# A gated recurrence and a long convolution on one core: scan on transposed inputs, 128x49 prime-factor convolution, batches overlapped

## The chip, the cores and the metric

The kernel runs on one core of one Trainium2 chip. The metric is the device time of a launch in microseconds (us). The times are medians of four executions (three in the first table of the kernel before); each execution also lists the core's span (from its first to its last instruction) and its mean granted TensorE clock, as a share of full speed. Engines: PE is TensorE, PEld its weight loads, DVE VectorE, ACT ScalarE, POOL GpSimd, SP SyncE.

## The reference

```python
# x, f_logit: (4, 6272, 256) f32; the weights are shared by the batches
f = lower_bound + (1 - lower_bound) * sigmoid(f_logit)
for t in range(6272):                      # recurrence in time
    h = f[:, t] * h + (1 - f[:, t]) * x[:, t]
    y[:, t] = h
x1, x2, x3 = split(y @ w_proj, 3)          # 256 columns each
conv = irfft(rfft(x2, axis=1) * rfft(filter_fft, axis=0))   # circular, length 6272
out = (x1 * conv * x3) @ w_out
```

6272 is 128 x 49, and 128 and 49 have no common factor. A Fourier transform of that length can therefore be done as a 128-point and a 49-point one, either with "twiddle" factors between them (Cooley-Tukey, the kernel before) or with the time index permuted and no twiddles (Good-Thomas, the change).

## The kernel before

Four batches, one after another, each in three stages. Recurrence: a chunk of 128 time steps is a cumulated product and a cumulated sum, done as triangular matmuls around Ln and Exp.

```python
def stage0(c):                  # cumulated log f, in both orientations
    nc.tensor.matmul(pL[:, 0, :], tri16n[:], logf_c, start=True, stop=True)
    nc.tensor.matmul(pL[:, 1, 0:128], logf_c[:, 0:128], tri16[:], start=True, stop=True)
    ...
def stage1(c):
    nc.scalar.activation(cc[:], pLs.pop(c)[:], AF.Exp)
    nc.vector.tensor_tensor(g[:], us[c], cc[:, 0, :], op=AOP.mult)
def stage2(c):
    nc.tensor.matmul(pP[:, 0:128], g[:, 0:128], tri32[:], start=True, stop=True)
    ...
        nc.vector.scalar_tensor_tensor(hT[j][:, c * T:(c + 1) * T], in0=pP[:, ...],
            scalar=sc, in1=cum[:, ...], op0=AOP.add, op1=AOP.mult)
    if c in seg:                # strided permutation of h
        nc.scalar.copy(hTp[kh][:, :, k0:k1],
                       hT[kh].rearrange("p (n1 e) -> p e n1", e=N2)[:, :, k0:k1])
```

Convolution, for each half of the channels: projection x2, 128-point transform with twiddles, PE transposes, 49-point transform, product with the filter's spectrum H, PE transposes, and the way back. Then gates and output.

```python
for j in range(2):
    ... # pj = x2 projection, pA = 128-point transform with twiddle tables
    for k1 in range(g0, g0 + gn):
        nc.tensor.transpose(pT[:98, k1 - g0, :], A_sb[:, :, :, k1], iden16[:])
    ... # pX = 49-point transform; six DVE operations a group for Y = X * H
    for k1 in range(g0, g0 + gn):
        nc.tensor.transpose(pT[:98, k1 - g0, :], Y[:, k1, :, :], iden16[:])
    for dl in range(g0, g0 + GD):
        nc.tensor.matmul(pB[:NK, dl - g0, :], Yt[:98, :, dl], W49I_hi[:98, :], ...)
    ... # pc: 128-point inverse, two matmuls for each of 49
for q0 in range(0, N2, 4):      # gates: 8 matmuls of 512 columns a group and half
    ...
for sb0 in range(NCH):          # output projection, 49 stores of 128 KB a batch
    ...
    nc.sync.dma_start(out[b, sb0::N2, :], osb[:])
```

Each stage opens its own pools of SBUF and PSUM and closes them, so a stage can begin only when the memory that it needs has been given back.

Of the kernel before, what the change touches and what calls it, by code (L numbers as in the profile page):

```python
# [9 lines left out]
F32 = mybir.dt.float32  # L11
# [3 lines left out]
AF = mybir.ActivationFunctionType  # L15

S = 6272
D = 256
N1 = 128
N2 = 49  # L20
NK = 65
T = 128
NCH = S // T
DJ = 768

_DBG = None
_NB = None


def _frac_sin(nc, pool, out_ap, psum_ap, denom, pi_col, npart, nfree):  # L30
    q = pool.tile([128, nfree], F32, tag="tg_q", name="tgq")
    nc.vector.tensor_scalar(q[:npart], in0=psum_ap, scalar1=1.0 / denom,
                            scalar2=None, op0=AOP.mult)
    qi = pool.tile([128, nfree], I32, tag="tg_qi", name="tgqi")
    nc.vector.tensor_copy(qi[:npart], q[:npart])
    qf = pool.tile([128, nfree], F32, tag="tg_qf", name="tgqf")
    nc.vector.tensor_copy(qf[:npart], qi[:npart])
    r = pool.tile([128, nfree], F32, tag="tg_r", name="tgr")
    nc.vector.scalar_tensor_tensor(r[:npart], in0=qf[:npart], scalar=-float(denom),
                                   in1=psum_ap, op0=AOP.mult, op1=AOP.add)  # L40
    f0 = pool.tile([128, nfree], F32, tag="tg_f0", name="tgf0")
    nc.vector.tensor_scalar(f0[:npart], in0=r[:npart], scalar1=1.0 / denom,
                            scalar2=None, op0=AOP.mult)
    f1 = pool.tile([128, nfree], F32, tag="tg_f1", name="tgf1")
    nc.vector.scalar_tensor_tensor(f1[:npart], in0=f0[:npart], scalar=0.0,
                                   in1=f0[:npart], op0=AOP.is_lt, op1=AOP.add)
    nc.scalar.activation(out_ap, f1[:npart], AF.Sin, bias=pi_col[:npart],
                         scale=(-2.0 * math.pi))
# [3 lines left out]
def kernel(  # L52
# [13 lines left out]
    if _NB is not None:  # L66
        B = _NB
    dbg = _DBG if _DBG is not None else {}

    konst = ctx.enter_context(tc.tile_pool(name="konst", bufs=1))  # L70
    tblp = ctx.enter_context(tc.tile_pool(name="tblp", bufs=1))
    hpool = ctx.enter_context(tc.tile_pool(name="hpool", bufs=1))

    tri32 = konst.tile([128, 128], F32, tag="tri32")
    make_upper_triangular(nc, tri32, 1.0, diag=True)
    tri16 = konst.tile([128, 128], F16, tag="tri16")
    nc.vector.tensor_copy(tri16[:], tri32[:])
    tri16n = konst.tile([128, 128], F16, tag="tri16n")
    nc.vector.tensor_scalar(tri16n[:], in0=tri32[:], scalar1=-1.0, scalar2=None,
                            op0=AOP.mult)  # L80
    iden16 = konst.tile([128, 128], F16, tag="iden16")
    make_identity(nc, iden16)
    pi_col = konst.tile([128, 1], F32, tag="pi_col")
    nc.vector.memset(pi_col, math.pi)

    lbrow = konst.tile([128, D], F32, tag="lbrow")
    nc.sync.dma_start(lbrow, lower_bound.unsqueeze(0).to_broadcast([128, D]))
    onemlb = konst.tile([128, D], F32, tag="onemlb")
    nc.vector.tensor_scalar(onemlb[:], in0=lbrow[:], scalar1=-1.0, scalar2=1.0,
                            op0=AOP.mult, op1=AOP.add)  # L90

    wp_hi = konst.tile([128, 2, DJ], F16, tag="wp_hi")
    wp_lo = konst.tile([128, 2, DJ], F16, tag="wp_lo")
    wo_hi = konst.tile([128, 2, D], F16, tag="wo_hi")
    wo_lo = konst.tile([128, 2, D], F16, tag="wo_lo")

    TBLA_hi = tblp.tile([128, N2, 130], F16, tag="TBLA_hi")
    TBLAI = tblp.tile([128, N2, 2, 128], F16, tag="TBLAI")
    W49F_hi = tblp.tile([128, 98], F16, tag="W49F_hi")
    W49F_lo = tblp.tile([128, 98], F16, tag="W49F_lo")  # L100
    W49I_hi = tblp.tile([128, 98], F16, tag="W49I_hi")
    W49I_lo = tblp.tile([128, 98], F16, tag="W49I_lo")
    H_sb = [hpool.tile([128, NK, N2, 2], F16, name=f"H_{j}", tag=f"H_{j}")
            for j in range(2)]

    with tc.tile_pool(name="t32", bufs=1) as t32p:
        TBLA32 = t32p.tile([128, N2, 130], F32, tag="TBLA32")
        W49F_f32 = t32p.tile([128, 98], F32, tag="W49F_f32")
        iden32 = t32p.tile([128, 128], F32, tag="iden32")
        make_identity(nc, iden32)  # L110
        wtmp = t32p.tile([128, 2, DJ + D], F32, tag="wtmp")
        nc.sync.dma_start(wtmp[:, :, 0:DJ], moe_w_proj.rearrange("(a p) j -> p a j", p=128))
        nc.sync.dma_start(wtmp[:, :, DJ:], moe_w_out.rearrange("(a p) j -> p a j", p=128))
        nc.vector.tensor_copy(wp_hi[:], wtmp[:, :, 0:DJ])
        nc.vector.tensor_copy(wo_hi[:], wtmp[:, :, DJ:])
        nc.vector.tensor_tensor(wp_lo[:], wtmp[:, :, 0:DJ], wp_hi[:], op=AOP.subtract)
        nc.vector.tensor_tensor(wo_lo[:], wtmp[:, :, DJ:], wo_hi[:], op=AOP.subtract)

        with tc.tile_pool(name="tgen", bufs=2) as tg, \
                tc.tile_pool(name="tgen1", bufs=1) as tg1, \  # L120
                tc.tile_pool(name="tgps", bufs=2, space=bass.MemoryType.PSUM) as tgps:
            def irow(n, pattern, base, name):
                t_i = tg1.tile([1, n], I32, name=name + "_i", tag=name + "_i")
                nc.gpsimd.iota(t_i[:], pattern=pattern, base=base, channel_multiplier=0)
                t_f = tg1.tile([1, n], F32, name=name + "_f", tag=name + "_f")
                nc.vector.tensor_copy(t_f[:], t_i[:])
                return t_f
            krow = irow(130, [[0, 2], [1, NK]], 0, "krow")
            orow = irow(130, [[1568, 2], [0, NK]], 1568, "orow")
            arow = irow(128, [[49, 128]], 0, "arow")  # L130
            ones256 = irow(256, [[0, 256]], 1, "ones256")
            ones128 = ones256[:, 0:128]
            ones98 = ones256[:, 0:98]
            for g0 in range(0, N2, 3):
                gn = min(3, N2 - g0)
                pv = tgps.tile([128, 3, 130], F32, tag="tgp", name="pv")
                for jj in range(gn):
                    n2 = g0 + jj
                    bcrow = tg.tile([1, 130], F32, tag="bcrow", name="bcrow")
                    nc.vector.scalar_tensor_tensor(bcrow[:], in0=krow[:], scalar=float(n2),  # L140
                                                   in1=orow[:], op0=AOP.mult, op1=AOP.add)
                    nc.tensor.matmul(pv[:, jj, :], arow[:], krow[:], start=True, stop=False)
                    nc.tensor.matmul(pv[:, jj, :], ones128[:], bcrow[:], start=False,
# [350 lines left out]
```

## Time and profile before

| | us |
|---|---|
| median of 3 runs | 2099.86 (2098.29 to 2106.0) |
| set-up (tables, filter spectrum) | 301 |
| a batch: recurrence, convolution with gates, output | 154 + 228 + 59 = 441, with joins 451 |

The prediction below shows the lines that carry this. The page also has a row for each engine with its busy share in 40 equal slices, in tenths. In these two rows of the kernel before the reader sees four blocks apart from one another: POOL works only where a recurrence runs; ACT reaches 6 or 7 in each of them and is mostly at 0 to 3 between (with a 5 or 6 now and then).

```profile
ACT  1000027671620356762321367635122476724203
POOL 0000023300000043200000063000000333000000
```

### The profile page before, as it was taken

The page shows a single profiled execution, that of the slowest core. Times are in us where ns is not written, and L with a number is a line of the kernel's source. Part 1 is how long each engine was busy: PE and PEld are TensorE (multiplying, and loading weights), DVE is VectorE, ACT ScalarE, POOL GpSimd, SP SyncE. Part 2 cuts the span into 40 slices and gives each one's busy share as a digit, 9 for nine tenths or more (in the row PEclk, how much of TensorE's full clock was granted, in tenths as well). Part 3 has the DMA queues.
Part 4 walks back from the last instruction along what each step waited for, and adds up shares of the span by engine and source line. Part 5 has one row for each costly group of instructions (what it writes and reads, how often), then busy time and mean ns, then how long its engine had stood idle before and what let it go on. Part 6 is the DMA issues. An engine that isn't in the chain of part 4 may idle for free.

```text
span 2097.7 us, 23892 instructions
## 1 busy us (share of the span) xinstructions
PE 1407.8 (67%) x8944; PEld 1081.2 (52%) x8944; DVE 1020.8 (49%) x2697; ACT 800.7 (38%) x1364; POOL 227.4 (11%) x68
## 2 busy tenths in 40 slices
PE   5869853566979624577889334578797335679795
PEld 5547553446765313456674233457664234467643
DVE  7744616637267036626465055553752156273660
ACT  1000027671620356762321367635122476724203
POOL 0000023300000043200000063000000333000000
PEclk9995655677758955686759856786678566867597
DMA  0021022200000342100001521000002421000003
GB/s 23 0 69 54 0 94 72 80 1 1 1 1 1 108 141 80 41 1 1 1 1 35 167 86 61 21 1 1 1 1 78 151 80 61 1 1 1 1 11 113
DMA packets 92549, 86.22 MB, mean 41 GB/s; under 512 B 3984, under 2 KB 92176, under 8 KB 92432
## 3 DMA queue, kind: packets, MB, share of 16 engines
q1 hardware_dynamic: 92432, 84.69, 12.6%
q8 instruction: 70, 1.15, 0.2%
q14 instruction: 47, 0.39, 0.1%
HBM read 58.98 MB, written 25.69 MB: 40 GB/s over the span
## 4 chain that ended last, share of the span: by engine, by line
PE 32%; ACT 23%; DVE 21%; issue 12%; DMA 10%; POOL 1%; ACTq 0%; SPq 0%; DVEq 0%; POOLq 0%
DMA out_dram<-osb 7%; DVE g L271 6%; ACT Th L409 6%; PE px L431 4%; ACT hTp L296 4%; PE pT L362 4%; PE px L443 4%; PE pj L338 3%; ACT x2c L341 3%; PE pP L278 2%; ACT Asb L351 2%; DVE Yt L400 2%; PE pc L414 2%; PE pc L416 2%; ACT osb L462 2%
## 5 line engine op out<-in xcount | busy, mean ns | idle before, releaser
L271 DVE TENSOR_TENSOR g<-xu,cc 128x256 f32<-128x256 f32 x196 | 194.5, 1005 | 394.2 <-ACT cc L268 392.0
L241 POOL TENSOR_TENSOR fw<-fw,onemlb 128x2048 f32<-128x2048 f32 (+1 forms) x24 | 110.3, 4595 | 1485.4 <-ACT fw L239 1485.4
L259 PE MATMUL pL<-logf,tri16n 128*128 128x256 f16 x196 | 72.8, 373 | 249.7 <-ACT cc L268 162.5
L409 ACT CAST Th<-pB 65x392 f16<-65x392 f32 x256 | 115.8, 481 | 315.9 <-PE pB L407 315.9
L462 ACT COPY osb<-po 128x256 f32<-128x256 f32 x196 | 72.1, 372 | 366.4 <-PE po L457 238.8
L278 PE MATMUL pP<-tri,g 128*128 128x128 f32 x392 | 129.2, 427 | 117.3 <-DVE g L271 114.7
L338 PE MATMUL pj<-wp_hi,hTp 128*128 128x256 f16 x784 | 152.8, 294 | 56.4 <-ACT x2c L341 34.8
L364 DVE COPY At<-pT 98x512 f16<-98x512 f16 (+1 forms) x136 | 55.4, 412 | 265.8 <-ACT x2c L341 140.6
L341 ACT CAST x2c<-pj 128x256 f16<-128x256 f32 x392 | 136.7, 388 | 110.9 <-PE pA L348 64.2
L457 PE MATMUL po<-wo_hi,cT 128*128 128x256 f16 x392 | 116.5, 315 | 81.3 <-ACT osb L462 81.3
L278 PEld LDWEIGHTS pP<-tri,g 128*128 128x128 f32 x392 | 91.3, 287 | 142.2 <-DVE g L271 137.6
L260 PEld LDWEIGHTS <-logf 128*128 128x128 f16 x196 | 25.0, 128 | 258.7 <-issue 256.5
L268 ACT ACTIVATE cc<-pL 128x512 f32<-128x512 f32 x196 | 109.3, 599 | 113.2 <-DVE hTs L288 104.4
L457 PEld LDWEIGHTS <-cT 128*128 128x128 f16 x784 | 86.7, 112 | 125.5 <-issue 103.9
L418 DVE CAST cT<-pc 128x512 f16<-128x512 f32 (+1 forms) x104 | 67.9, 659 | 145.4 <-PE pc L416 145.4
L338 PEld LDWEIGHTS <-hTp 128*128 128x128 f16 x784 | 80.9, 109 | 99.8 <-issue 65.1
L288 DVE SCALAR_TENSOR_TENSOR hTs<-pP,hlast,cc 128x128 f16<-128x128 f32 x384 | 130.6, 340 | 0.0
L373 PE MATMUL pX<-W49F_hi,At 98*128 98x98 f16 x520 | 80.4, 257 | 66.2 <-DVE xht L388 66.2
L407 PE MATMUL pB<-W49I_hi,Yt 98*65 98x98 f16 x1024 | 117.3, 308 | 6.2 <-DVE Yt L400 6.2
L247 POOL TENSOR_TENSOR xu<-xu,fw 128x2048 f32<-128x2048 f32 (+1 forms) x24 | 113.6, 4735 | 65.7 <-DVE hTs L288 32.6
L296 ACT COPY hTp<-hTs 128x1568 f16<-128x1568 f16 x32 | 111.7, 3541 | 22.5 <-DVE hTs L288 22.5
L407 PEld LDWEIGHTS <-Yt 98*65 98x65 f16 x1024 | 116.0, 206 | 7.5 <-DVE Yt L400 7.5
(134 smaller groups left out, 3233.2 us busy)
## 6 DMA issues: line engine op xcount, KB each, us to landing
out_dram<-osb SPq DMA_DIRECT2D x196, 128.0 KB, 1.7
xu<-in_x_dram SPq DMA_DIRECT2D x20, 1024.0 KB, 5.5
fw<-in_f_logit_dram SPq DMA_DIRECT2D x20, 1024.0 KB, 5.5
ffsb<-in_moe_filter_fft_dram SPq DMA_DIRECT2D x2, 3136.0 KB, 12.3
xu<-in_x_dram SPq DMA_DIRECT2D x4, 1152.0 KB, 6.2
fw<-in_f_logit_dram SPq DMA_DIRECT2D x4, 1152.0 KB, 9.0
wtmp<-in_moe_w_proj_dram SPq DMA_DIRECT2D x1, 768.0 KB, 6.4
wtmp<-in_moe_w_out_dram SPq DMA_DIRECT2D x1, 256.0 KB, 6.7
```

The costliest lines, as they stand in the source:

```text
L241: nc.gpsimd.tensor_tensor(fw[:, 0:nq, :], fw[:, 0:nq, :], onemlb[:].unsqueeze(1).broadcast_to([128, nq, D]), op=AOP.mult)
L247: nc.gpsimd.tensor_tensor(xu[:, 0:nq, :], xu[:, 0:nq, :], fw[:, 0:nq, :], op=AOP.mult)
L271: nc.vector.tensor_tensor(g[:], us[c], cc[:, 0, :], op=AOP.mult)
L278: nc.tensor.matmul(pP[:, 0:128], g[:, 0:128], tri32[:], start=True, stop=True)
L288: nc.vector.scalar_tensor_tensor(hT[j][:, c * T:(c + 1) * T], in0=pP[:, j * 128:(j + 1) * 128], scalar=sc, in1=cum[:, j * 128:(j + 1) * 12 ...
L296: nc.scalar.copy(hTp[kh][:, :, k0:k1], hT[kh].rearrange("p (n1 e) -> p e n1", e=N2)[:, :, k0:k1])
L338: nc.tensor.matmul(pj[:], hTp[kh][:, n2, :], wp_hi[:, kh, D:2 * D], start=(kh == 0), stop=(kh == 1))
L341: nc.scalar.copy(x2c[:], pj[:])
L407: nc.tensor.matmul(pB[:NK, dl - g0, :], Yt[:98, :, dl], W49I_hi[:98, :], start=True, stop=True)
L409: nc.scalar.copy(Th[:NK, g0:g0 + GD, :, :], pB[:NK, 0:GD, :])
L457: nc.tensor.matmul(po[:], yT[kh][:, sb0, :], wt_[:, kh, :], start=first, stop=(kh == 1 and wt_ is wo_lo))
L462: nc.scalar.copy(osb[:], po[:])
```

## The change

Its intent: replace the triangular matmuls by one DVE scan over time on transposed chunks of 392 steps; drop twiddles and all f16 transposes by the prime-factor order; give every stage its own memory for the whole program, and issue the recurrence of batch b+1 alternately with the 16 spectral "units" of batch b (a unit is 8 pairs of channel groups: px on PE, two products p0, p1 and two sums Y on DVE, inverse pi on PE, eviction Th on ACT). Core of the diff, cut and with some lines shortened ("..."):

```diff
-def stage0(c): / stage1(c): / stage2(c):      # Ln, Exp, triangular matmuls
+def hgrn(b):
+    for c in range(NCHK):                      # 16 chunks of 392 steps
+        nc.sync.dma_start(xt[:TB], x[b, t0:t0 + CH, :]...)
+        nc.sync.dma_start(ft[:TB], f_logit[b, t0:t0 + CH, :]...)
+        nc.scalar.activation(ft[:TB], ft[:TB], AF.Sigmoid, scale=-1.0)
+        nc.gpsimd.tensor_tensor(xt[:TB], xt[:TB], ft[:TB], op=AOP.mult)
+        for kh in range(2):
+            ... # 4 f32 transposes each into sT (ft) and uT (xt)
+            nc.scalar.activation(fT[:], sT[:, 0:CH], AF.Identity, scale=nomc..., bias=1.0)
+            nc.vector.tensor_tensor_scan(h32[:], fT[:], uT[:, 0:CH], last, op0=mult, op1=add)
+            nc.gpsimd.tensor_copy(hG[b][:, kh, :, c * MR:(c + 1) * MR],
+                                  h32[:].rearrange("p (m r) -> p r m", r=Q))
...
+# set-up: the filter, row by row, evicted with a step of 49 elements
+    nc.scalar.copy(vh[:, p, :, :, q], src)
+    nc.vector.tensor_tensor(vl[:, p, :, :, q], src, vh[:, p, :, :, q], op=AOP.subtract)
...
+def units(b):
+    for u in range(NU):                        # 16
+        px = psx.tile([128, 2, 512], F32, name="px", tag="X")          # one buffer
+        ... # 4 matmuls of 512 columns
+        nc.vector.tensor_tensor(p0[:TB], px[:TB], H[:TB, :, u, :], op=AOP.mult)
+        nc.vector.tensor_tensor(p1[:TB], px[:TB], H[:TB, ::-1, u, :], op=AOP.mult)
+        nc.vector.tensor_tensor(yf[:TB, 0], p0[:TB, 0], p0[:TB, 1], op=AOP.subtract)
+        nc.vector.tensor_tensor(yf[:TB, 1], p1[:TB, 0], p1[:TB, 1], op=AOP.add)
+        nc.gpsimd.tensor_copy(Y[:TB, :, :, 0], zm[:TB, :, es])
+        pi = psm.tile([128, 2, 512], F32, name="pi", tag="m")          # two buffers
+        ... # 8 matmuls of 196 columns
+        nc.scalar.copy(dst, src)                                       # pi -> Th
...
+for b in range(B):
+    weave((seq(phase_p(b), phase_f1(b)), 13 + NU), (phase_z(b), 26))
+    mini(b)                                    # the DC and Nyquist rows
+    if b + 1 < B:
+        weave((units(b), NU), (hgrn(b + 1), NCHK))
+    else:
+        run(units(b))
+    run(phase_o(b))
```

The pool psm (tag m, two buffers of two banks) serves pr, pp, pa, p13, pi, pc and po.

## The prediction

> **What bounds the kernel now.** I read the busy shares on the page first, then the chain that ended last, then a table of stages, then the groups, and last a few microseconds of timeline to get spacings.
>
> ```profile
> span 2097.7 us, 23892 instructions
> ...
> PE 1407.8 (67%) x8944; PEld 1081.2 (52%) x8944; DVE 1020.8 (49%) x2697; ACT 800.7 (38%) x1364; POOL 227.4 (11%) x68
> ...
> PEclk9995655677758955686759856786678566867597
> ...
> PE 32%; ACT 23%; DVE 21%; issue 12%; DMA 10%; POOL 1%; ACTq 0%; SPq 0%; DVEq 0%; POOLq 0%
> ```
>
> No engine is full, and the chain changes engine all the time: nothing sets the end alone. The stages one after another do. The chain shows the starts of four equal batches at 301, 742, 1193 and 1645 us, so 301 us of set-up and about 451 us for a batch. Busy time by stage, for set-up and batch 0 (recurrence, convolution with gates, output):
>
> ```profile
> 0.00:301.00 301.00, 231.65 (x892) 175.21 (x893) 165.03 (x509) 15.44 (x22) 3.93 (x20) 0.79 0.12 38
> 301.00:455.00 154.00, 70.48 (x369) 56.02 (x369) 87.22 (x245) 105.76 (x97) 55.90 (x12) 0.63 0.19 59
> 455.00:683.00 228.00, 187.99 (x1432) 147.30 (x1431) 124.02 (x296) 70.34 (x190) 0.00 (x0) 0.73 0.00 1
> 683.00:742.00 59.00, 34.32 (x215) 22.41 (x214) 2.83 (x7) 18.00 (x49) 0.00 (x0) 0.88 0.32 108
> ```
>
> The columns are the stretch, PE, PEld, DVE, ACT, POOL, granted clock, DMA share and GB/s. The recurrence (154 us) uses PE for 46% of the time and POOL works only there; the convolution (228 us) is PE at 82% with a clock of 0.73; the output (59 us) waits for 128 KB stores. Batches hardly overlap, which is the first thing the change is after.
>
> ```profile
> L271 DVE TENSOR_TENSOR g<-xu,cc x196: 404/418/4725, 313.8 to 1797.4; 128x256 f32<-128x256 f32 x196
> ```
>
> That is all of its instructions, minimum, median and maximum in ns; the timeline beside POOL's:
>
> ```profile
> 311.90 4.50 POOL L241 TENSOR_TENSOR fw<-fw,onemlb 128x2048 f32<-128x2048 f32 x1 [0.33 <-ACT fw L239]
> 313.82 7.84 DVE L271 TENSOR_TENSOR g<-xu,cc 128x256 f32<-128x256 f32 x3 [24.78 <-ACT cc L268]
> 316.48 4.57 POOL L247 TENSOR_TENSOR xu<-xu,fw 128x2048 f32<-128x2048 f32 x1
> ```
>
> The multiply g takes 0.42 us in the median, but up to 4.7 us: three of them take 7.84 us while POOL runs two long multiplies, because the second waits for POOL to end each time.
>
> ```profile
> L407 PEld LDWEIGHTS <-Yt 98*65 98x65 f16 x1024 | 116.0, 206 | 7.5 <-DVE Yt L400 7.5
> ...
> L296 ACT COPY hTp<-hTs 128x1568 f16<-128x1568 f16 x32 | 111.7, 3541 | 22.5 <-DVE hTs L288 22.5
> L268 ACT ACTIVATE cc<-pL 128x512 f32<-128x512 f32 x196 | 109.3, 599 | 113.2 <-DVE hTs L288 104.4 <-PE pP L280 5.1 <-PE pL L262 3.3
> ...
> L362 PEld LDWEIGHTS <-Asb 128*98 128x98 f16 x520 | 94.4, 267 | 4.6 <-issue 2.2 <-ACT Asb L351 2.1
> ...
> L247 POOL TENSOR_TENSOR xu<-xu,fw 128x2048 f32<-128x2048 f32 x20 | 93.5, 4673 | 65.4 <-DVE hTs L288 32.6 <-DMA xu<-in_x_dram 32.5
> ...
> L338 PEld LDWEIGHTS <-hTp 128*128 128x128 f16 x784 | 80.9, 109 | 99.8 <-issue 65.1 <-ACT hTp L296 25.4
> ...
> L437 DVE TENSOR_TENSOR cT<-px,cT 128x512 f16<-128x512 f32 x96 | 66.2, 690 | 25.2 <-PE px L431 25.2
> ```
>
> Strided weights load in 206 to 267 ns, contiguous ones in 109. The strided ACT copy costs 3541/1568 = 2.3 ns an element. The other three rows are prices that I use below.
>
> [...]256-column matmuls start every 0.213 us in one part of the output stage and every 0.108 in another, 512-column ones every 0.216 at full clock.[...]
>
> **The change part by part.** Removed: Ln and Exp with their triangular matmuls, and the table loads that they force (88 of 1.283 us, 113 us of ACT in all); all 1040 f16 transposes on PE with strided weights; the 1024 + 784 small inverse matmuls, replaced by 512 and 784; the second projection of x2 (it was computed once for each half of d); the strided copies hTp; 144 of 196 stores (52 remain, mostly of 512 KB). Unchanged in size: the gate projections (x1 and x3) and the output projection.
>
> Spacing rather than duration sets throughput: back-to-back DVE and ACT instructions start about 0.08 us sooner than the previous one ends (0.40 us long, 0.32 apart). From 690 ns at 512 columns[...], a 1024-column DVE read of PSUM is 1.22 us long, 1.14 apart; a 1024-column ACT copy, from 599 ns and 0.83 ns a column, 1.03 long, 0.95 apart.
>
> Set-up: trigonometry on DVE, about 8 tables of 6 operations of 0.3 us plus casts, 25 us. 49 f32 rotations, each two passes of 256 columns; a 128-column f32 pass took 0.213 us in the recurrence, so 0.85 cold and 0.43 warm; PSUM eviction by ACT and DVE, two each of about 0.25 us, keeps to the same pace: 32 us. 16 filter units, 24 matmuls of 128 columns at 0.08 to 0.107 and 12 of 512 at 0.216: about 5 us, 80 in all. Recurrence of batch 0: 256 f32 transposes at about 0.2 us (those of the present set-up ran at 0.33 with DVE waits between) is 51 us of PE, of which I hide half. 25 + 32 + 80 + 25, with 23 for Hm, pool change and stalls: 185 us.
>
> Projection, first transform and gates of a batch: gates 192 matmuls of 512 and 16 of 128 columns, as now, 43 us in the stretch from 640 to 683 at clock 0.91; x2 98 × 0.108 = 11; transform 128 × 0.081 (the 98-column pairs are 0.081 apart) to 0.107 = 10 to 14. PE 66. ACT 26 × 0.5 + 13 × about 1.3 + 8 × 0.95 = 38, DVE 26 × 0.61 + 8 × 1.14 = 25, POOL's 97 rotating copies at about 0.3 (a 128-element POOL instruction takes 0.29) = 29: all beside PE. Only two PSUM buffers are shared by three users; 12 us for that: 78 us. The Nyquist step (mini): 4 us, exposed.
>
> Spectral units with the next recurrence, a unit and a chunk at a time. PE at a clock of 0.7: four of 512 at 0.3, eight of 196 at 0.125, sixteen transposes at 0.2: 1.2 + 1.0 + 3.2 = 5.4 us. DVE: two products 2.28, two f16 sums of 512 about 0.34 each, [...]the sums have two SBUF inputs and POOL is busy more than half the time, so I add 1.2: 6.0. POOL: a multiply of 1024 columns, half of 4673 ns, 2.3[...], plus the small Nyquist copy, 0.3. ACT: 0.95 + 2 × 0.5 + about 1.0 = 3. So DVE and PE are close, and each hands over to the other (products wait for PE, inverse matmuls wait for DVE and POOL, the uT buffer waits for the scan): 7.9 us a pair, 126 us a batch, three times. The last batch has no recurrence to overlap: with one px buffer, 1.3 on PE, then 2.28 and 0.5 of handing over, 4.2 us, 67 in all.
>
> Output: pc 196 matmuls at 0.06 to 0.107, po 196 × 0.108: 12 to 21 + 21 = 37 us of PE; per group of four, two PSUM buffers each held about 5.7 us together, so 2.8 us a group at best; with waits 3.5: 46 us. Stores of 512 KB in that time are about 140 GB/s, which the present stage reaches without trouble.
>
> Sum: 185 + 4 × 78 + 4 × 4 + 3 × 126 + 67 + 4 × 46 + 20 for joins between stages = 1162; I say 1160 us.
>
> **The rivals.** First, the overlapped stage becomes a chain: [...]nothing overlaps within a pair and it takes 12 us rather than 7.9: 3 × 66 = 197 us more, about 1360. For it: [...]there is a single px buffer. Against: in the present trace x2 projections of the second half run between transposes of the first (L338 inside the L362 run at 483 us), so the framework does reorder to fill gaps. Second, strided eviction by ACT: x2 and Th are written in runs of four and read with a step; at the 2.3 ns an element of hTp they would take 2.4 and 1.8 us, hidden beside PE and DVE in the overlapped stage, but about 15 us a batch exposed in the projection stage: 1220. Against: DVE reads pX with a step of two at full speed. Third, the clock stays warm and PSUM hand-over is cheap: projection and gates 70, pair 6.2, output 41, set-up 165: about 1000. Fourth, no gain, because PE's gate and output work (about 65 us a batch) is unchanged and slow parts move to POOL; POOL would have to reach 25 us a pair for that, five times my price.
>
> **Range and chances.** The optimistic sum is 1000, the chain 1360, strided ACT 1220. Errors of stages partly cancel; unmeasured prices (scan, POOL copies, f32 transposes) are all in the overlapped stage, so the upper side is wider: 1030 to 1310. Even the slowest of these takes 35% less time than now, so faster 0.985, same 0.01, slower 0.005.
>
> **What would show it right or wrong.** The first convolution of batch 0 should begin near 185 us rather than 455, and batches should be about 255 us apart. [...]a transpose 0.15 to 0.25 apart, [...]x2 evictions near 1.05 (2.4 for the second rival). The f16 sums should show medians near 0.42 us and a long tail beside POOL. In the overlapped stage PE and DVE should both be 65 to 80% busy; one of them under 50% with the pair near 12 us is the first rival. The prediction is wrong if set-up exceeds 230 us, if a stage is bound by POOL or ACT, or if the gate stage drops below a clock of 0.8.

Prices that no trace or run shows are terms of the sum, the price of the scan on DVE and that of the permuting copy on POOL. With them DVE came to 6.0 us a pair and POOL to 4.8; the 7.9 us a pair, the 126 a batch and the sum of 1162 rest on DVE's 6.0.

The 1024-column prices agree with the kernel before: cT (L437) on DVE takes 0.287 us for 128 columns and 0.690 for 512 (1.05 ns a column), the sigmoid fw on ACT 1.910 us for 2048 and 2.122 for 2304 (0.83 ns a column); the changed kernel's products take 1.22 us and its copies osb 1.02. The multiplies of pX, read with a step of two, took 0.40 us for 245 columns, as did the sums Y of the same size without a step. Full clock is 1.00 granted from 682.8 to 687.0 us (512 columns every 0.216 us, 256 every 0.108), half is 0.50 from 692.3 to 693.8 (256 every 0.213). The 1.2 us added for the sums is the estimate from the multiply g; in the changed kernel's first overlapped stage the sums, with both inputs in SBUF, lasted up to 2.57 us while POOL worked, the products, which read px from PSUM, never over 1.23.

## The result

| kernel | median us | range | runs |
|---|---|---|---|
| before | 2102.7 | 2098.29 to 2106.0 | 4 |
| after | 1227.76 | 1226.48 to 1228.79 | 4 |

The ratio is 0.5842 (95% interval 0.583 to 0.5854). Every ratio here is the mean time of one kernel's runs over that of the other's of the same rounds, so it isn't quite the ratio of the medians quoted. The predicted 1160 was 68 us too low; the range 1030 to 1310 holds it.

The page of the changed kernel: instructions fell from 23892 to 14846, the chain that ended last still changes engines, but PE now has 46% of it, and stores are no longer among its lines.

```profile
span 1227.1 us, 14846 instructions
...
PE 892.4 (73%) x5784; PEld 577.3 (47%) x5784; DVE 639.7 (52%) x806; ACT 504.3 (41%) x649; POOL 386.8 (32%) x701
...
PEclk9996599999955569999755579998655799995579
...
PE 46%; DVE 28%; POOL 9%; ACT 8%; issue 7%; DMA 3%; POOLq 0%; SPq 0%; DVEq 0%; ACTq 0%
```

The clock row is in tenths of full speed, 40 slices. From the twelfth slice on it goes down to 5 four times: in the three stages where units and the next recurrence run together, and near the end where the last units run alone. The busy time by stage (stretch, length, PE, PEld, DVE, ACT, POOL, clock, DMA share, GB/s), for set-up, gates of batch 0, units with the recurrence of batch 1, output of batch 0, and the last batch's units:

```profile
0.00:240.00 240.00, 169.86 (x984) 115.15 (x984) 139.40 (x250) 147.85 (x205) 93.12 (x110) 0.89 0.35 102
240.00:331.00 91.00, 67.40 (x436) 37.14 (x436) 26.41 (x35) 41.85 (x55) 24.16 (x100) 0.98 0.00 1
331.00:444.00 113.00, 87.50 (x408) 59.09 (x410) 93.85 (x97) 39.06 (x55) 66.38 (x101) 0.54 0.32 93
444.00:501.00 57.00, 39.74 (x437) 30.47 (x436) 18.86 (x18) 19.11 (x22) 25.41 (x60) 0.86 0.41 145
...
1100.00:1174.00 74.00, 51.34 (x194) 26.08 (x196) 50.11 (x69) 12.99 (x16) 4.05 (x16) 0.51 0.00 0
```

Set against the terms of the prediction's sum (all from the records of the stages' first and last instructions; a gate stage ends here with its last product z, so the DVE part of the Nyquist step, about 3 us, lies in the row of the units, beside their start):

| stage | predicted | measured | difference |
|---|---|---|---|
| set-up with recurrence 0 | 185 | 240.1 | +55 |
| gates and Nyquist step, four | 4 x 82 = 328 | 91.5 + 3 x 88.4 = 357 | +29 |
| units with recurrence, three | 3 x 126 = 378 | 112.3 + 114.2 + 112.7 = 339 | -39 |
| last units alone | 67 | 73.5 | +6 |
| outputs, joins and end | 4 x 46 + 20 = 204 | 57.6 + 57.4 + 49.4 + 49.5 + 3.6 = 218 | +14 |
| sum | 1162 | 1227 | +65 |

The groups that carry the prices (engine, operation, out<-in, count, busy us, mean ns, then idle before and what ended it):

```profile
L138 DVE TENSOR_TENSOR_SCAN h<-fT,h,uT 128x392 f32<-128x392 f32 x120 | 120.6, 1024 | 11.2 <-PE uT L132 7.1 <-ACT f2h L297 4.1
L143 POOL CAST hG<-h 128x392 f16<-128x392 f32 x128 | 109.6, 861 | 359.9 <-PE p L406 262.2 <-DVE h L138 95.8
L297 ACT CAST f2h<-pr 128x128 f16<-128x128 f32 x98 | 68.0, 766 | 36.0 <-PE pr L293 25.1 <-DVE f2l L298 8.5
L370 ACT CAST x<-pp 128x1024 f16<-128x1024 f32 x48 | 67.8, 1412 | 14.3 <-PE pp L368 14.3
L451 DVE TENSOR_TENSOR Y<-p 98x512 f16<-98x512 f16 x64 | 67.6, 1056 | 0.0
L298 DVE TENSOR_TENSOR f2l<-pr,f2h 128x128 f16<-128x128 f32 x98 | 67.3, 745 | 26.8 <-ACT f2h L297 24.8
L450 DVE TENSOR_TENSOR Y<-p 98x512 f16<-98x512 f16 x64 | 34.3, 535 | 0.0
```

The scan takes 1.02 us. The filter evictions f2h and f2l take 0.75 us for 128 elements, which nothing in the prediction allowed for. The two sums Y do the same amount of work and last 0.42 us when nothing is in their way (the last batch: 415 and 418 ns); their means of 0.54 and 1.06 carry the waits behind POOL.

### The profile page after: what moved, and what is told of

It reads as the page before. It is cut to its first block, busy times and chain, and to the rows that moved or that the text cites. A ratio compares the mean times of both kernels' runs of the same rounds, so it can differ in the third digit from the quotient of the medians. Undisturbed runs are those within 1.5% of the kernel's fastest.

```text
span 1227.1 us, 14846 instructions
## 1 busy us (share of the span) xinstructions
PE 892.4 (73%) x5784; PEld 577.3 (47%) x5784; DVE 639.7 (52%) x806; ACT 504.3 (41%) x649; POOL 386.8 (32%) x701
## 4 chain that ended last, share of the span: by engine, by line
PE 46%; DVE 28%; POOL 9%; ACT 8%; issue 7%; DMA 3%; POOLq 0%; SPq 0%; DVEq 0%; ACTq 0%
PE p L406 15%; PE po L491 8%; PE px L442 5%; DVE z L482 4%; DVE p L446 4%; DVE z L412 4%; DVE Y L451 4%; ACT x1s L411 4%; PE pfx L324 3%; PE pr L293 3%; DVE A L386 3%; DVE h L138 3%; POOL hP L366 3%; POOL xt L123 3%; PE pc L478 2%
## 5 line engine op out<-in xcount | busy, mean ns | idle before, releaser
L143 POOL CAST hG<-h 128x392 f16<-128x392 f32 x128 | 109.6, 861 | 359.9 <-PE p L406 262.2
L406 PE MATMUL p<-hG,W13h 128*128 128x512 f16 (+1 forms) x416 | 150.3, 368 | 83.2 <-DVE z L412 42.5
L123 POOL TENSOR_TENSOR xt<-xt,ft 98x1024 f32<-98x1024 f32 x64 | 157.4, 2461 | 131.5 <-DMA xt<-in_x_dram 54.9
L406 PE MATMUL p<-hG,W13l 128*128 128x512 f16 (+1 forms) x416 | 150.3, 367 | 0.0
L132 PE MATMUL uT<-iden,xt 98*128 98x98 f32 x512 | 107.2, 353 | 53.5 <-ACT fT L135 27.9
L491 PE MATMUL po<-Woh,z 128*128 128x256 f16 x392 | 99.3, 294 | 55.1 <-DVE z L482 53.2
L442 PE MATMUL px<-A,FT 98*128 98x512 f16 x256 | 118.9, 593 | 27.0 <-DVE p L447 20.4
L138 DVE TENSOR_TENSOR_SCAN h<-fT,h,uT 128x392 f32<-128x392 f32 x120 | 120.6, 1024 | 11.2 <-PE uT L132 7.1
L128 PE MATMUL sT<-iden,ft 98*128 98x98 f32 x512 | 105.3, 352 | 19.4 <-ACT ft L122 16.0
L491 PE MATMUL po<-Wol,z 128*128 128x256 f16 x392 | 98.6, 292 | 0.0
```

What stands on the lines that cost most here:

```text
L123: nc.gpsimd.tensor_tensor(xt[:TB], xt[:TB], ft[:TB], op=AOP.mult)
L128: nc.tensor.transpose(sT[:, j * TB:(j + 1) * TB], ft[:TB, j, cols], iden[:TB, :TB])
L132: nc.tensor.transpose(uT[:, j * TB:(j + 1) * TB], xt[:TB, j, cols], iden[:TB, :TB])
L138: nc.vector.tensor_tensor_scan(h32[:], fT[:], uT[:, 0:CH], 0.0 if last[kh] is None else last[kh][:, CH - 1:CH], op0=AOP.mult, op1=AOP.add)
L143: nc.gpsimd.tensor_copy(hG[b][:, kh, :, c * MR:(c + 1) * MR], h32[:].rearrange("p (m r) -> p r m", r=Q))
L406: nc.tensor.matmul(p13[:, i, 0:cn], w[:, kh, js], hG[b][:, kh, r0:r0 + rn, :], start=(n == 0), stop=(n == 3))
```

## Experiments

Twelve kernels ran, all gave correct results. Stages are measured as in the table above. The first eight test the parts of the change and the prediction's terms; the last four ask what bounds what is left.

### scan_only: the recurrence of the change in the kernel before

```diff
-            # stage0/1/2: Ln, Exp, triangular matmuls, strided copy hTp on ACT
+            # the chunk loop of hgrn(b), writing the old hTp layout, in the old pools
```

> The kernel before with nothing but its recurrence replaced by the scan of the new one (transposed chunks of 392, one lower-bound factor folded into the weights); set-up, convolution and output stay. Theory: alone, a chunk is paced by GpSimd (2.46 for the multiply and twice 0.86 for the permuting copies, 4.2 us), so a batch's recurrence takes about 75 to 85 us in place of 154, and the kernel 1800 to 1840. Rival: with two buffers of each load the chunk is a serial chain (load 3, sigmoid 1.05, multiply 2.4, transposes and scans 3) of 7 us, 112 to 120 us a batch: 1930 to 1960.

Measured: 1761.22 us (1755.52 to 1769.25), ratio 0.839 (0.836 to 0.842). Both theories missed. The rival was right about the chunk: alone, a recurrence takes 106 us for 16 chunks, 6.6 us each, and in the stretch from 290 to 380 us no engine is over 60% busy:

```profile
290.00:380.00 90.00, 43.49 (x212) 33.33 (x212) 26.65 (x26) 32.11 (x43) 53.34 (x40) 0.50 0.43 125
```

It is a chain through POOL's multiply, transposes, ACT, scan and copy. But batches are 354 us apart instead of 451, because the recurrence now runs almost wholly beside the output of the batch before: its permuting copies go from 634 to 740 us, the evictions of that output from 633 to 754. The two together take 121 us where, one after the other, the recurrence took 106 us here and an output about 56 in the kernel before. The recurrence's redesign alone is worth 338 us of the 875, part of it by overlap that I hadn't planned.

### serial: the change without overlap of batches

```diff
-            weave((units(b), NU), (hgrn(b + 1), NCHK))
+            run(units(b))
+            run(phase_o(b))
+            tc.strict_bb_all_engine_barrier()
+            run(hgrn(b + 1))
+            tc.strict_bb_all_engine_barrier()
```

> The new kernel with the recurrence of the next batch moved behind the output stage, between two barriers, so that it overlaps nothing. Theory: units alone take 73 us as in the last batch, the recurrence alone 75 to 85 plus barriers, together about 45 us a batch more than the 113 of the overlapped stage: 1350 to 1370, so the overlap is worth about 130 us, a small part of the 875 gained. The f16 sums of the units should then all last 0.42 us, because GpSimd is idle beside them. Rival: the overlapped stage is held up by shared limits so much that overlap buys under 50 us: below 1280.

Measured: 1448.5 us (1447.86 to 1451.06), ratio 0.69 (0.6885 to 0.6916): overlap is worth 221 us, more than both theories said. The parts alone, units and recurrence:

```profile
329.00:397.00 68.00, 48.86 (x183) 24.84 (x184) 47.43 (x65) 11.37 (x14) 3.81 (x15) 0.51 0.00 0
460.00:566.00 106.00, 52.30 (x256) 40.32 (x256) 32.84 (x32) 34.93 (x48) 63.58 (x48) 0.50 0.39 113
```

The first stretch ends with the last px; with the last inverse and its eviction (to 402 us) the units alone take 73 us, as the theory said. So 73 and 106 us apart, 113 together. The 221 us also hold what the barriers cost: from the last eviction of an output (452 us) to the first multiply of the recurrence (462 us) the engines stand and the first loads come in. I had expected the recurrence alone to be faster; as a chain with no engine over 60%, it fits into the gaps of the units and they into its own. The step from scan_only to serial, 313 us, is the new convolution and set-up, less the overlap that scan_only had and serial forbids.

### rot4: filter evictions four rows at a time

```diff
-                nc.scalar.copy(vh[:, p, :, :, q], src)
-                nc.vector.tensor_tensor(vl[:, p, :, :, q], src, vh[:, p, :, :, q], ...)
+            # pr holds four rows; rows q0 to q0+3 are neighbours in the destination
+                nc.scalar.copy(vh[:, p, :, :, q0:q0 + qn], src)
+                nc.vector.tensor_tensor(vl[:, p, :, :, q0:q0 + qn], src, ...)
```

> The new kernel with the filter's rotated rows evicted four at a time (26 ACT copies and 26 DVE subtractions of 512 elements in runs of four f16, in place of 98 and 98 of 128 elements that write single f16 at a step of 98 bytes); the filter rows are loaded one by one, in that order. Theory: set-up overran by 55 us because each of those evictions lasts 0.75 us, not the 0.25 that I priced; with 26 of about 0.8 set-up falls from 240 to about 200 and the kernel to about 1188. Rival: set-up is paced by the recurrence of batch 0 beside it (its last chunk ended at 176 us), so less than 10 us is gained: above 1215.

Measured: 1181.81 us (1177.51 to 1184.69), ratio 0.5633 (0.5617 to 0.5648), 46 us less than the changed kernel. The edit also loads the filter's rows one by one and hands out set-up in more portions beside the recurrence. In its groups, 512 elements now cost nearly what 128 did:

```profile
L297 DVE TENSOR_TENSOR f2l<-pr,f2h 128x512 f16<-128x512 f32 x24 | 19.8, 856 | 13.0 <-ACT f2h L296 12.9
L296 ACT CAST f2h<-pr 128x512 f16<-128x512 f32 x24 | 19.2, 825 | 19.0 <-PE pr L292 11.8 <-DVE f2l L297 6.9
```

The rotations end at 83 us instead of 155, and set-up at 184 us: the predicted 185. (56 us less; the gate stage that follows became 8 us longer, 99.8, and gave some of it back.) The theory holds: the term that failed in set-up is the price of these evictions. The number of elements isn't that price, and a fixed cost of each instruction isn't either: in the kernel before, a DVE copy of 128 neighbouring elements from PSUM (At_f) took 0.29 us in the mean, these take 0.75. That 184 meets the predicted 185 is partly luck, since the prediction had tables and rotations done after 57 us, not 83.

### psum3: a third PSUM buffer in the gate and output stages

The two banks of the pool psx are idle in both stages.

```diff
-                p13 = psm.tile([128, 2, 512], F32, name="p13", tag="m")
+                p13 = (psx.tile([128, 2, 512], F32, name="p13x", tag="X") if jb else
+                       psm.tile([128, 2, 512], F32, name="p13", tag="m"))
...
-            pc = psm.tile([128, 2, 512], F32, name="pc", tag="m")
+            pc = (psx.tile([128, 2, 512], F32, name="pcx", tag="X") if (r0 // 4) % 2 else
+                  psm.tile([128, 2, 512], F32, name="pc", tag="m"))
```

> The new kernel with the third pair of PSUM banks, idle in these stages, used as a further buffer for every second gate product and every second output spectrum. Theory: PE waits about 20 us a batch for evictions in the gate stage because three users share two buffers; two thirds of it goes, and about 3 us of the output stage: 1160 to 1175. Rival: the waits are for the evicting engines themselves (x1s on ACT before z on DVE), so the buffer changes less than 10 us: above 1217.

Measured: 1089.23 us (1084.54 to 1097.43), ratio 0.5191 (0.5165 to 0.5218), 139 us less. The direction is the theory's, the size over twice what I expected. The gate stage and the output stage of batch 0 in this kernel's table of stretches:

```profile
239.00:306.00 67.00, 63.07 (x434) 36.56 (x434) 27.24 (x36) 41.58 (x55) 24.89 (x101) 0.97 0.00 1
...
419.00:467.00 48.00, 37.63 (x424) 29.89 (x421) 17.37 (x17) 16.59 (x18) 20.39 (x58) 0.87 0.39 149
```

67 us where 91 were, with PE busy 94% of it: the gate stage is now bound by its matmuls, and the third buffer removed 24 to 27 us a batch of waits for evictions. The output stages go from 49 to 57 us down to 37 to 49. The overlapped stage, which the edit doesn't touch, stays at 112 to 114.

### lock: the permuting copy hG on ACT instead of POOL

```diff
-                nc.gpsimd.tensor_copy(
+                nc.scalar.copy(
                     hG[b][:, kh, :, c * MR:(c + 1) * MR], ...
```

> The new kernel with the permuting copy of each scan's result moved from GpSimd to ACT. Theory: VectorE bounds the overlapped stage (85 to 90% busy), and part of that is blocking by GpSimd: beside the recurrence the two f16 sums last 0.53 and 1.06 us in the mean, alone 0.42 and 0.42, 0.75 us a unit, 12 us a batch. Without the copies GpSimd is busy 2.6 instead of 4.3 us a pair, so about 40% of that goes: 3 batches of 5 us, 1205 to 1218. Rival: the order of instructions or PE sets the stage, or ACT's strided reads (1 us or more each) become a new wait: 1228 or slower.

Measured: 1211.09 us (1209.04 to 1214.25), ratio 0.5766 (0.5751 to 0.5781), 17 us less, as the theory said. The sums in this kernel's groups:

```profile
L451 DVE TENSOR_TENSOR Y<-p 98x512 f16<-98x512 f16 x64 | 33.4, 522 | 0.0
L450 DVE TENSOR_TENSOR Y<-p 98x512 f16<-98x512 f16 x64 | 29.8, 465 | 0.0
```

Their busy time fell from 102 to 63 us; the sums themselves are 64 x 0.833 = 53. So POOL's copies had blocked DVE for 39 us over three stages, yet the stages shortened by only 4 to 5 us each (112.3, 114.2, 112.7 to 108.6, 108.8, 108.4), 13 in all. The other two thirds lay beside other waits, or were taken back by the copies' work on ACT; this run doesn't tell which. The copy (392 elements read with a step of 196 bytes) has nearly the same price on ACT (878 ns) as on POOL (861, and POOL's records are rough), 2.2 ns an element.

### ysum: the sums folded into the inverse matmuls

```diff
-            nc.vector.tensor_tensor(yf[:TB, 0], p0[:TB, 0], p0[:TB, 1], op=AOP.subtract)
-            nc.vector.tensor_tensor(yf[:TB, 1], p1[:TB, 0], p1[:TB, 1], op=AOP.add)
...
-                nc.tensor.matmul(o, Y[:TB, 0, ...], VA[:TB], start=True, stop=False)
-                nc.tensor.matmul(o, Y[:TB, 1, ...], VB[:TB], start=False, stop=True)
+                # 16 instead of 8 matmuls a unit: p0 with VA and -VA, p1 with VB and VB
+                nc.tensor.matmul(o, y[:TB, r, ...], v[:TB], start=(n == 0), stop=(n == 3))
```

> The new kernel without the two f16 sums on VectorE: the inverse matmuls take the four products themselves (16 matmuls of 196 columns a unit in place of 8, with the negative of one table), and the Nyquist columns are copied into the products. Theory that VectorE bounds the overlapped stage: 0.7 us of sums and 0.75 of blocking go, VectorE needs 4.4 us a pair instead of 6.2, PE at half clock 1.3 us more (7.3 a pair), so the gain is real only if the fuller PE is granted full clock: then 113 becomes about 85 us a batch and the kernel about 1130. If PE stays at half clock it becomes the bound: 110 to 118 us a batch, 1220 to 1250. The last batch's units alone should lose 5 to 10 us either way.

Measured: 1238.44 us (1234.41 to 1240.2), ratio 0.5892 (0.5877 to 0.5908), in the range of "the clock stays half", but the stages say otherwise. Batch 1 with a recurrence, then the last batch:

```profile
582.00:686.00 104.00, 77.53 (x566) 58.51 (x568) 69.22 (x67) 45.68 (x62) 69.97 (x113) 0.85 0.42 117
...
1074.00:1182.00 108.00, 74.16 (x324) 42.71 (x326) 38.53 (x35) 12.99 (x16) 6.97 (x32) 0.53 0.00 0
```

With a recurrence beside it the clock rose to 0.85 and the stage fell from 114 to 104 us; without, the clock stayed at 0.53 and the units went from 73.5 to 108 us. A gain of 7 to 12 us three times and a loss of 35 us once, with small gains and losses elsewhere (the outputs of batches 0 and 1 took 3 us more each), make the total. My expectation took the two cases as one.

### px2: the spectrum matmuls done twice

```diff
-            for o, terms in (...):
-                for n, (tb, r) in enumerate(terms):
+            for rep in range(2):
+              for o, terms in (...):
+                for n, (tb, r) in enumerate(terms):
```

> The new kernel with the four spectrum matmuls of each unit done twice (the second run overwrites the first with the same numbers). If VectorE bounds the overlapped stage: PE has room for half of the 1.7 us (half clock), so 0 to 10 us a batch there and 14 to 27 in the last batch, 1245 to 1290. If PE's half clock is the bound: 27 us a batch, 1330 or more. If the added activity brings full clock: 1210 to 1240.

Measured: 1262.65 us (1259.69 to 1265.89), ratio 0.6011 (0.5994 to 0.6027). Again the total hides two cases: the overlapped stages became shorter although PE has 64 more large matmuls in each (105.3, 110.5, 110.1 us), at a clock of 0.83 to 0.89, and the last batch's units went from 73.5 to 113 us.

```profile
333.00:439.00 106.00, 76.84 (x501) 50.68 (x500) 84.03 (x101) 45.21 (x62) 70.02 (x98) 0.89 0.41 114
```

So the number of PE's matmuls doesn't bind the overlapped stage of the changed kernel. PE's time isn't ruled out: because the clock rose, its busy time in the first of these stages fell from 87.5 to 76.8 us although it had more to do. The busy share alone doesn't give the clock: PE was busy for 72% of this stage at a clock of 0.89, and for 77% of the changed kernel's at 0.54. The sums were also blocked less here (means 625 and 417 ns), so how much of the 3 to 7 us is the clock and how much the blocking, this run can't say.

### rot4_psum3: both

The two edits above together.

> The new kernel with both the batched rotation evictions and the third buffer. Theory: the two gains (46 and 139 us) belong to different stages and add up: 1035 to 1050. Rival: they share a limit: 1065 or more.

Measured: 1042.77 us (1041.05 to 1046.52), ratio 0.4965 (0.4948 to 0.4982). The gains add: 46 + 139 = 185, and 1228 - 185 = 1043. Gate stages 67.2, 62.6, 62.6, 61.6 (predicted 78 without the Nyquist step), set-up 185.5 (predicted 185).

### combo: with the copy on ACT as well

rot4, psum3 and lock together.

> The wide filter evictions, the third PSUM buffer and the permuting copy on ACT together. Theory (the lock between DVE's f16 sums and POOL's copies costs the overlapped stage its own 5 to 6 us a batch, whatever the other stages do): 1042.8 less the 16.7 us that the ACT copy gave alone, 1026 us (1020 to 1032), each of the three overlapped stages 113 to 116 us before and 106 to 109 after. Rival (with the other two edits the overlapped stage has slack elsewhere, or ACT becomes its bound): 1036 us or more.

Measured: 1009.74 us (1004.39 to 1017.56), ratio 0.4809 (0.4783 to 0.4835), 33 us less than rot4_psum3 instead of 17. The overlapped stages are 120.4, 108.2 and 107.2 us (117.1, 116.1, 115.3 before), 13 us less in all, and set-up and gates are as before. The rest came from where I wasn't looking: the outputs of batches 0 and 1 fell from 49.2 and 50.4 to 37.2 each. (The stages are those of the profiled run, the fastest of the four, 39 us below that of rot4_psum3.) Those waits are already in the changed kernel: in the output stage of batch 0, from 448 to 470 us, PE and DVE wait for a recurrence (engine, what it waits for, us, times, longest):

```profile
PEld uT L132 <- POOL xt L123: 6.4, 1, 6.4
PE uT L132 <- POOL xt L123: 6.2, 1, 6.2
DVE h L138 <- PE uT L132: 6.0, 1, 6.0
```

and the timeline of those microseconds tells why:

```profile
452.74 3.31 POOL L364 COPY hP<-hG 128x110 f16<-128x110 f16 x18
...
457.72 4.64 POOL L123 TENSOR_TENSOR xt<-xt,ft 98x1024 f32<-98x1024 f32 x2
460.11 0.61 PEld L132 LDWEIGHTS uT<-iden,xt 98*128 98x128 f32 x4 [6.36 <-POOL xt L123]
```

The transposes uT belong to the first chunks of the recurrence after next (batch 2's) and stand among the output matmuls in PE's stream. They wait for POOL's multiply, which runs only after POOL's rotating copies hP for batch 1. No output matmul starts in that time either: PE is idle from 453.9 to 460.1 us, then does the transposes and goes on with po at half clock (0.50 granted from 460 to 466 us, one every 0.21 us) until 466. The same stands in the output of batch 1 (PE idle from 716.3 to 720.4), and not in those of batches 2 and 3, which have no later recurrence. By these traces it accounts for most of the difference between the 57.5 us of the first two outputs in the changed kernel and the 49.4 of the other two. The stages show the difference: rot4_psum3 first, then combo, where that wait no longer appears.

```profile
370.00:418.00 48.00, 37.45 (x427) 30.09 (x424) 17.37 (x17) 16.24 (x18) 20.67 (x58) 0.87 0.39 146
```

```profile
372.00:410.00 38.00, 34.52 (x431) 28.54 (x431) 17.27 (x17) 18.34 (x22) 19.23 (x54) 0.98 0.51 188
```

In the run lock the wait is still in the trace (PE idle from 445.4 to 451.5 us before such a transpose), and its outputs stayed at 57.7 and 56.6 us; in combo PE's longest pause in this stage is 0.8 us. Why moving a copy off POOL removed the wait here and not there stays open.

### combo_px: a second buffer for px

In the last batch of the changed kernel a unit is a loop of 4.33 us. Its timeline (start, length, engine, line; in brackets the idle time before and what ended it):

```profile
1122.78 1.89 PE L442 MATMUL px<-A,FT 98*128 98x512 f16 x4 [1.14 <-DVE p L447]
...
1124.70 1.23 DVE L446 TENSOR_TENSOR p<-px,H 98x1024 f16<-98x1024 f32 x1 [1.32 <-PE px L442]
...
1125.84 1.22 DVE L447 TENSOR_TENSOR p<-px,H 98x1024 f16<-98x1024 f32 x1
...
1127.12 1.89 PE L442 MATMUL px<-A,FT 98*128 98x512 f16 x4 [1.14 <-DVE p L447]
```

px can be written only after both products have read it, and the products wait for px.

```diff
-            px = psx.tile([128, 2, 512], F32, name="px", tag="X")
+            px = (psm.tile([128, 2, 512], F32, name="pxm", tag="m") if u % 2 else
+                  psx.tile([128, 2, 512], F32, name="px", tag="X"))
```

> As the previous kernel, and every second spectral unit takes its px from the PSUM pool that pi uses, so that px of unit u+1 can be written while DVE still reads px of unit u. Theory (a unit is a loop through the one px buffer: 1.9 us of matmuls at half clock, then 2.4 us of products, 4.33 us in the last batch of the changed kernel): the last batch's units fall from 74 us to about 16 times DVE's 3.0, near 50 us, and the overlapped stages lose about 8 us each, in all 46 us: 980 us (970 to 992). Rival A (the loop binds only the last batch; beside a recurrence DVE's queue or the half clock binds): 22 to 26 us less, 1000 to 1004. Rival B (pi and px now fight for two buffers, nothing is gained): 1020 or more.

Measured: 1031.57 us (1023.93 to 1036.5), ratio 0.4907 (0.4881 to 0.4932), 22 us slower than combo; rival B. The last batch's units grew from 74.5 to 88.2 us, and two overlapped stages from 108 to 116; the first became shorter (120.4 to 113.6). Two units now took 10.1 us. Its timeline (start, length in us, engine, line, operation; in brackets the idle time before and what ended it):

```profile
921.30 1.77 PE L443 MATMUL pxm<-A,FT 98*128 98x512 f16 x4
...
926.60 0.35 PE L458 MATMUL pi<-VA,Y 98*128 98x196 f16 x1 [3.53 <-POOL Y L453]
...
928.45 1.87 PE L443 MATMUL px<-A,FT 98*128 98x512 f16 x4 [0.36 <-DVE p L448]
```

The next pxm starts at 931.42. Its buffer had been free since ACT evicted pi at 928.94, but in PE's queue pxm stands behind px and behind the pi of the other unit. The loop is now pxm, products, sums, pi, px, pi, pxm: longer than two loops of one buffer. The buffer shared with a later step of the same chain didn't decouple anything here; it fixed an order.

### combo_px_y: sums in the matmuls where a recurrence runs beside

combo_px with the edit of ysum in batches 0 to 2; the last batch keeps its sums.

```diff
+            if b + 1 < B:
+                terms4 = ((y0, 0, VA), (y0, 1, VAn), (y1, 0, VB), (y1, 1, VB))
+            else:
+                ... # the two sums on DVE
+                terms4 = ((Y, 0, VA), (Y, 1, VB))
```

> As the previous kernel, and the f16 sums are folded into the inverse matmuls (16 instead of 8 a unit) in the three batches that have a recurrence beside them; the last batch keeps the sums. Theory (DVE's queue with its sums binds the overlapped stage; with more matmuls the clock rises as it did to 0.83 in the run without sums): each overlapped stage 5 to 8 us shorter, 15 to 24 us in all below the previous kernel. Rival (PE binds the overlapped stage once px has two buffers, at half clock 8 more matmuls of 0.164 us are 21 us a batch): slower than the previous kernel by 15 us or more. Within 8 us of it: neither binds, and loads or POOL do (POOL would then be above 75% busy, or ACT would wait for ft's DMA).

Measured: 966.39 us (961.34 to 968.9), ratio 0.4604 (0.4588 to 0.4619), 65 us less than combo_px, far beyond the theory's 15 to 24. The overlapped stages went from 113.6, 116.5, 115.9 to 94.8, 91.9, 89.6 us at a clock of 0.81 to 0.87. Batch 1's stage, combo_px first:

```profile
467.00:582.00 115.00, 87.97 (x417) 58.99 (x417) 80.08 (x95) 63.97 (x86) 43.35 (x75) 0.55 0.34 95
```

```profile
448.00:538.00 90.00, 72.18 (x530) 54.01 (x531) 61.95 (x60) 59.34 (x82) 43.78 (x89) 0.81 0.40 113
```

The rival's forecast (21 us a batch slower) is wrong: PE got 128 more matmuls a batch and the stage became shorter. But the rival assumed half clock. With the clock up, PE's busy time fell by 16 us and DVE's by 18, so the run doesn't say which of the two made the stage shorter; nor does any run tell what these sums bring without the shared px buffer. The last batch, with the sums, remained at 87.6 us.

### best: two loops taken apart

In the last batch the odd px goes to the two single banks of the recurrence's transposes, idle there; and x's chunks get three buffers.

```diff
+            two = b + 1 == B and u % 2
+            if two:
+                px = [pst.tile([128, 512], F32, name="pxt", tag="t") for _ in range(2)]
...
-            xt = hg.tile([128, NBLK, D], F32, name="xt", tag="xt")
+            xt = hg.tile([128, NBLK, D], F32, name="xt", tag="xt", bufs=3)
```

> The 966 us kernel with two edits that lie in different stages, so that each is read from its own stage. First, in the last batch the odd units take px from the two one-bank PSUM buffers of the recurrence's transposes, which are idle there, instead of from pi's buffers. Theory (one px buffer makes the unit a loop of 1.9 us of matmuls and 2.4 us of products; sharing with pi tied pxm behind the pi of the unit before and made 5.2 us of it): the last batch's units go from 84 us (70 with one buffer) to DVE's own 3.1 us a unit, 48 to 55 us. Rival (the order of PE's queue or the half clock holds it): 65 us or more. Second, three buffers for the x chunks instead of two. Theory (loads of x hold the recurrence: POOL's multiply waits for that DMA 4 to 8 us in each overlapped stage, a chunk late each time): overlapped stages from 90 to 93 us down to 84 to 88. Rival (the loads are late but something else would hold it then): 90 to 93 as before. Both theories: 915 to 928 us in all; the first alone 930 to 938; none 955 or more.

Measured: 944.19 us (939.39 to 946.53), ratio 0.4486 (0.4464 to 0.4508); the fastest kernel. Each edit is read from its own stage. The last units took 54.7 us from the end of the gate stage to the first output matmul (87.6 before), so the first theory holds. DVE's timeline in this kernel shows no pause, two units in 6.0 us:

```profile
869.45 1.21 DVE L461 TENSOR_TENSOR p<-px,H 98x1024 f16<-98x1024 f32 x1
870.58 1.21 DVE L462 TENSOR_TENSOR p<-px,H 98x1024 f16<-98x1024 f32 x1
871.71 0.41 DVE L472 TENSOR_TENSOR Y<-p 98x512 f16<-98x512 f16 x1
872.04 0.41 DVE L473 TENSOR_TENSOR Y<-p 98x512 f16<-98x512 f16 x1
872.38 2.47 DVE L458 TENSOR_TENSOR p<-pxt,H 98x512 f16<-98x512 f32 x4
```

The second theory fails: POOL's wait for x's loads disappeared, but the overlapped stages are 100.4, 98.9 and 101.7 us, slower than before, not faster. Counted with the output stages, which became 1 to 5 us shorter, they lost 3, 2 and 11 us. What took the loads' place isn't settled; POOL's multiply now waits for ACT's sigmoid instead (26.5 us in the first of these stages), and PE's busy time there rose from 70.9 to 77.0 us. The kernel with the first edit alone would be some 16 us faster by an estimate from these three numbers; it wasn't run.

## Why the prediction was right, and where it was off

**Direction and size.** Right: batches 260 us apart (predicted 255) and 240 of set-up (185). The chance of 0.985 for faster was safe: serial shows that even without overlap the time would have been 1448.

**Set-up, +55: the step that failed.** "PSUM eviction by ACT and DVE, two each of about 0.25 us, keeps to the same pace: 32 us" is the term; it measured 0.766 and 0.745 us an eviction and 143 us for the stretch, all of it beside the recurrence. I priced 128 elements as if they lay side by side; they are written 98 bytes apart. rot4 shows the difference: with runs of four f16 the price fell from 6.0 to 1.6 ns an element on ACT (128 elements in 0.766 us, 512 in 0.825) and from 5.8 to 1.7 on DVE (0.745 and 0.856). Why the step costs this, no run shows. The prediction's own last part named 230 us as the limit above which it would be wrong; on this step it was. The other step of set-up held: 16 filter units in 80 us (157.8 to 238.0), for 80.

**Gates, +29: buffers.** The working had PE at 66 us and "12 us for that", two buffers for three users. PE was right: 65.5 busy us. The waits measured 23 us, nearly twice the term; psum3 took them away. (The 4 us for the Nyquist step were mostly not needed: it ran beside its neighbours.) The records put them down to PE waiting for the evictions z (42.5 us over four batches) and A (33.9). The mechanism was named and its size halved. The second rival, strided ACT, was half right on the price (1.41 us for x2, between 1.05 and 2.4) and wrong on the place: psum3's gate stage has the same evictions and no trouble with them. Strided eviction did cost time in set-up, where I hadn't looked.

**Overlapped stage, -39.** The first rival (a chain of 12 us a pair) is refuted: 7.1 us, below my 7.9. PE and DVE were 77% and 83% busy in that of batch 0 (I said 65 to 80). Prices: transposes 0.165 us apart (predicted 0.2); scan 1.02 us, 0.94 apart in a pair, and the permuting copy 0.86 us (only one length of scan was run, so its rate and fixed cost can't be told apart). PE's busy time for a unit and a chunk, 87.5/16 = 5.5 us, is the 5.4 priced, but by two errors that cancel: the clock was 0.54 and not 0.7, and the transposes were cheaper. DVE's, 93.9/16 = 5.9, is the 6.0 priced, in which the term for the scans is contained. So the mis-sized term is the handing over between them: 1.9 us on top of the busier engine in the prediction, 1.2 measured. The locks: 1.2 us a unit predicted, and over the three stages the sums lost 48.5 us, 1.0 a unit. But lock shows that removing four fifths of that gives back only a third. What binds this stage isn't settled. The chain that ended last goes through it from engine to engine (590 to 704 us of the changed kernel: issue 14%, loads of x 12%, and no line of PE, DVE or POOL over 11%), so no single engine's work explains it alone. ysum, px2 and combo_px_y made it shorter with more matmuls, but in each of them the clock rose and PE's busy time fell, so these runs don't separate the clock from the waits on DVE; no run raised the clock alone.

**Last units, +6.** 4.33 us a unit for 4.2 predicted, the same loop as described; best shows the loop by breaking it. The sum inside is luck in part: PE took 1.9 us for the predicted 1.3, at half clock (0.51 granted in this stage), and handing over almost nothing for the predicted 0.5. (The terms as written, 1.3 + 2.28 + 0.5, make 4.1, not 4.2.)

**Output, +14.** 46 predicted; 49.4 where nothing else interferes, and 57.5 in the two stages where a recurrence two batches ahead blocks PE's queue. The prediction had no such step: it treated the weave as confined to its stage. This cause is read from traces, and combo agrees, but no run removed that wait alone. The prediction also read too much into the kernel before: its output stage moved 108 GB/s, not 140; the changed kernel's moved 145, loads included, so nothing came of it.

**One reading of the kernel before.** The prediction says of three multiplies g that the second waits for POOL each time. By the trace the first two do: they last 2.86 and 4.72 us and end just after POOL's two multiplies; the third takes 0.41. The sense is the same.

## What to carry to other kernels

Price an eviction by where its elements land, not by their number alone (on ACT 128 elements 98 bytes apart took 0.77 us, 512 in runs of four 0.83); and when a stage looks PE-bound, ask what a third PSUM buffer would do before anything else, since here two idle banks were worth 139 us (the gate stages looked full of matmuls at 65.5 of 88.4 us). A second buffer that is shared with a later step of the same chain can lengthen the loop (combo_px, last batch: 74.5 to 88.2 us): look at the order in the engine's stream, for here one group of transposes that waited for another stage held up the output matmuls behind it for 6 us. Read a total by its stages: ysum and px2 each looked like a small loss and were a gain in three stages and a larger loss in one.
